# Segment 0 of a recurrent attention runs beside its weight loads, and batched V rows are spread over the segments

## The chip, the cores and the metric

The kernel runs on one core of a Trainium2 chip. The metric is the device time of one execution in microseconds (us); lower is better. The engines are named as in the profile: PE (matrix multiply, with PEld for its weight loads), DVE (vector), ACT (activation), POOL (GpSimd) and SP (which here only issues DMAs).

## What is computed

```python
# A: S = 2048 rows of width 512, in 64 segments of 32; 32 heads of 128; a memory of 8 rows
for s in range(64):
    h = concat(mem, layernorm(x)[s*32:(s+1)*32])            # 40 rows
    q, k, v = h @ Wq, h @ Wk, h @ Wv                          # each 512 -> 32 heads x 128
    p = softmax(where(mask, q @ k.T * 128**-0.5, -1e9))
    o = concat_heads(p @ v) @ Wo                              # 4096 -> 512
    mem, out[s] = o[:8], o[8:]
h = x + out
# B: a gated mixer over all 2048 rows
z = gelu(layernorm(h) @ w_in); z1, z2 = halves(z)
result = h + (z1 * (w_sp @ layernorm(z2) + b_sp)) @ w_out
```

All tensors are bf16. The memory that a segment hands on makes the 64 segments a recurrence.

## The kernel before

**The order of the work.** The program is written out by hand as one list of operations for each engine, by an `Emitter`. `Emitter.add` (L51) derives the waits from the named tokens that an operation reads and writes, and an engine runs its list in program order. Every DMA has a semaphore, and a wait on a DMA is a wait for its landing. For POOL there is one more dependence, on whatever stands before it on POOL:

```python
if eng == "pool" and self.by_eng["pool"]:
    deps.add(self.by_eng["pool"][-1])
```

**The weights.** Wq, Wk, Wv and Wo are 4 MB each and are loaded at the start, in this order, as four transfers of 1 MB each (a quarter holds eight heads), all issued by SP.

**Batched rows.** The last 8 rows of a segment's 32 are handled apart from the 24 rows before them: their q, k and v do not depend on the memory, so they are computed for a chunk of 16 segments at a time (128 rows). `qkx_mm` (L370) makes one group of four heads of q (groups 0 to 7) or k (groups 8 to 15), 16 matmuls of 128x128 into one PSUM bank, and `qkx_evac` (L382) copies it to `QTx`. `vx_mm` (L391) makes one of eight V rows of a chunk, 16 matmuls of which four run side by side, and `vx_evac` (L401) copies it to one of two staging buffers `Vs` and stores it to `vext_d` in DRAM. `load_vx` (L412) brings a segment's part of it back into `Vx` (three buffers). The four chunks hold segments 0 to 15, 16 to 31, and so on; `hTe` holds the transposed, normalized rows of two chunks.

**A segment** (the loop over `s`, L764). `QK` (L430) makes q and k of the 24 fresh rows and the 8 memory rows, 64 matmuls, and ACT and DVE bring them into place; `S_half` (L463) makes the scores with the mask added on PE, needing `qx_copy` (L455), which POOL makes for the next segment; then follow exp on ACT, `V_half` (L525), the sums and the logarithm and second exp that stand for a division, `PV_half` (L542), which needs `Vx`, `cT_evac` (L563), the output projection `Wo` (L575) in two column parts, `part_evac` (L592) and `mem_out` (L596), which puts the new memory into `hT` for the next segment's `QK`. `cTx_copy` (L586) is POOL's. `WoX_mm`, `F_group` and `WoX_scatter` finish a block of four segments one block later. One piece of the transpose of `w_sp` is fetched and written back (`wT_piece`, L669) in every second segment.

**Fillers.** Matmuls of later chunks are put in between. `gx` holds the groups of `qkx_mm`, one per segment, poured ahead of `PV_half`. `gv` holds V rows cut into pieces of four matmuls, four to a row; they are poured in eight of 16 segments (those in `VXS`, L745), one ahead of `Wo`, two ahead of `mem_out`, one behind it.

**The start** (L673 to L714). Two blocks of batched rows (chunks 0 and 1) are loaded first, normalized (`ln_inplace`, L331: two DVE operations, two of POOL, one of DVE) and transposed by PE. The 16 groups of chunk 0 follow as Wq and Wk arrive, with the first two blocks of x loaded, normalized and transposed after group 7, behind `late_consts` (L303), 35 POOL operations that build the mask and other constants. Then come the eight V rows of chunk 0, with stores issued by ACT, the loads of `Vx` for segments 0 and 1, and the segment loop. After the segments the mixer runs, which the change does not touch.

Of the kernel before, what the change touches and what calls it, by code (L numbers as in the profile page):

```python
# [33 lines left out]
class Emitter:  # L34
    ENGS = ("pe", "act", "dve", "pool", "sp")

    def __init__(self, n_dma_sems=16):
        self.ops = []
        self.by_eng = {e: [] for e in self.ENGS}
        self.last_w = {}  # L40
        self.readers = {}
        self.n_dma_sems = n_dma_sems
        self.dma_rr = 0
        self.dma_cnt = [0] * n_dma_sems
        self.dma_last = [None] * n_dma_sems
        self.const_tokens = set()
# [4 lines left out]
    def add(self, eng, fn, reads=(), writes=(), dma=False, after=()):  # L51
        op = _Op(eng, fn)
        deps = set(a for a in after if a is not None)
        for t in reads:
            w = self.last_w.get(t)
            if w is not None:
                deps.add(w)
            if isinstance(t, tuple) and t[0] == "ps":
                for r in self.readers.get(t, ()):
                    if r.eng != eng:  # L60
                        deps.add(r)
        for t in writes:
            w = self.last_w.get(t)
            if w is not None:
                deps.add(w)
            rs = self.readers.get(t)
            if rs:
                deps.update(rs)
        if eng == "pool" and self.by_eng["pool"]:
            deps.add(self.by_eng["pool"][-1])  # L70
        if eng == "pe":
            deps = {d for d in deps if d.eng != "pe" or d.is_dma}
        if dma:
            j = self.dma_rr
            self.dma_rr = (self.dma_rr + 1) % self.n_dma_sems
            op.is_dma = True
            op.dma_sem = j
            self.dma_cnt[j] += 1
            op.dma_val = 16 * self.dma_cnt[j]
            if self.dma_last[j] is not None:  # L80
                deps.add(self.dma_last[j])
            self.dma_last[j] = op
        op.deps = deps
        for t in reads:
            if t in self.const_tokens:
                continue
# [74 lines left out]
def fast_path(nc, st, keep, A_x, A_mem0, A_Wq, A_Wk, A_Wv, A_Wo, A_seg_len, B_w_in, B_w_sp, B_b_sp, B_w_out, out):  # L161
# [45 lines left out]
    hTe = sb("hTe", [128, 2, DC, 128], BF)  # L207
# [69 lines left out]
    def load_x(rb, j):  # L277
        sp(lambda e: e.dma_start(xn[:, j, :], xr[:, rb, :]), writes=[("xn", j)])

    def load_xe(ck, j):  # L280
        sp(lambda e: e.dma_start(xn[:, j, :], xe[CK * ck:CK * ck + CK, XM:SEG, :]), writes=[("xn", j)])
# [9 lines left out]
    load_xe(1, 1)  # L291
    for hq in range(4):
        load_w(0, hq)
    sp(lambda e: e.dma_start(m0[:], A_mem0[0]), writes=["m0"])
# [36 lines left out]
    def ln_inplace(j):  # L331
        dve(lambda e: e.bn_stats(out=st1[:, j, :], in_=xn[:, j, :]), reads=[("xn", j)], writes=[("st1", j)])
        dve(lambda e: e.bn_aggr(out=mv1[:, j, :], in_=st1[:, j, :]), reads=[("st1", j)], writes=[("mv1", j)])
        pool(lambda e: e.tensor_scalar(out=rs1[:, j:j + 1], in0=mv1[:, j, 1:2], scalar1=EPS, scalar2=None, op0=ALU.add),
             reads=[("mv1", j)], writes=[("rs1", j)])
        pool(lambda e: e.tensor_tensor(out=rs1[:, j:j + 1], in0=rs1[:, j:j + 1], in1=mhalf[:, 0:1], op=ALU.pow),
             reads=[("rs1", j), "mhalf"], writes=[("rs1", j)])
        dve(lambda e: e.tensor_scalar(out=xn[:, j, :], in0=xn[:, j, :], scalar1=mv1[:, j, 0:1], scalar2=rs1[:, j:j + 1],
                                      op0=ALU.subtract, op1=ALU.mult),
            reads=[("xn", j), ("mv1", j), ("rs1", j)], writes=[("xn", j)])  # L340

    def xT(j, bank):
        for dc in range(DC):
            pe(lambda e, dc=dc: e.transpose(out=psb[:, bank, dc * 128:(dc + 1) * 128], in_=xn[:, j, dc * 128:(dc + 1) * 128],
                                            identity=ident[:, :]),
               reads=[("xn", j), "ident"], writes=[PB(bank)])
# [10 lines left out]
    def xe_copy(ck, bank):  # L357
        src = psb[:, bank, 0:512].rearrange("p (dc c) -> p dc c", dc=DC)
        act(lambda e: e.activation(out=hTe[:, ck % 2, :, :], in_=src, func=ACT.Copy), reads=[PB(bank)], writes=[("hTe", ck % 2)])
# [10 lines left out]
    def qkx_mm(ck, i, bank, only_hh=None, only_dc=None):  # L370
        mi, h0 = i // 8, 4 * (i % 8)
        ws = (w_q, w_k)[mi]
        for hh in range(4):
            h = h0 + hh
            for dc in range(DC):
                if only_hh is not None and (hh, dc) != (only_hh, only_dc):
                    continue
                pe(lambda e, h=h, dc=dc, hh=hh: e.matmul(ps[:, bank, hh * 128:(hh + 1) * 128], lhsT=ws[:, dc, h * DH:(h + 1) * DH],  # L378
                                                         rhs=hTe[:, ck % 2, dc, :], start=(dc == 0), stop=(dc == DC - 1)),
                   reads=[("hTe", ck % 2), ("W", mi, h // 8)], writes=[PB(bank)])  # L380
# [10 lines left out]
    def vx_mm(ck, n, bank, only=None):  # L391
        for dc in range(DC):
            if only is not None and dc != only:
                continue
            for c in range(4):
                q = slice(32 * c, 32 * c + 32)
                pe(lambda e, dc=dc, c=c, q=q: e.matmul(ps[q, bank, :], lhsT=hTe[:, ck % 2, dc, q], rhs=w_v[:, dc, n * 512:(n + 1) * 512],  # L397
                                                       start=(dc == 0), stop=(dc == DC - 1), tile_position=(0, 32 * c)),
                   reads=[("hTe", ck % 2), ("W", 2, n // 2)], writes=[PB(bank)])

    def vx_evac(ck, n, bank, eng="act", queue="sp"):  # L401
        j = n % 2
        if eng == "act":
            act(lambda e: e.activation(out=Vs[:, j, :], in_=ps[:, bank, :], func=ACT.Copy), reads=[PB(bank)], writes=[("Vs", j)])
# [326 lines left out]
    gx, gv = Gap(), Gap()  # L731

    def qkx_atoms(ck, i):
        mms = [lambda ck=ck, i=i, hh=hh, dc=dc: qkx_mm(ck, i, XB, hh, dc) for hh in range(4) for dc in range(DC)]
        f = lambda: qkx_evac(ck, i, XB, "dve")
        f.eng = "dve"
        gx.add(XB, mms, f)
# [26 lines left out]
    for s in range(NSEG):  # L764
        j4 = s % 4
        rb = s // 4
        ck, i16 = s // CK + 1, s % CK
        if ck < NCK:
            if i16 == 0:
                for n in range(8):  # L770
                    vx_atoms(ck, n)
            qkx_atoms(ck, i16)
# [4 lines left out]
        if s % 2 == 0 and s // 2 < NWT:  # L777
# [3 lines left out]
        if i16 == 11 and 2 <= ck + 1 < NCK:  # L781
            load_xe(ck + 1, 1)
# [22 lines left out]
        sm_rcp(0)  # L805
        V_half(s, 1, (0, 1, 2))
# [12 lines left out]
        ev = gx.pour(16)  # L819
        PV_half(s, 0)  # L820
        PV_half(s, 1)
        cT_evac(0, "act")
# [9 lines left out]
        vx = i16 in VXS  # L832
        late = gv.pour(vx)
# [11 lines left out]
        if i16 == 12 and 2 <= ck + 1 < NCK:  # L845
            ln_inplace(1)
        late += gv.pour(2 * vx)
# [24 lines left out]
    assert not gx.atoms and not gv.atoms  # L872
# [922 lines left out]
```

## Time and profile before

| | us |
|---|---|
| median of 10 runs | 940.42 (938.7 to 943.83) |
| profiled execution, its own time | 940.29 |
| its span | 938.5 |
| PE busy in the span | 881.9 (94%) |
| ACT, DVE, POOL busy | 478.2, 445.3, 108.6 |
| last store of chunk 0's V rows issued | 54.7 |
| first QK of segment 0, 1, 63 | 50.02, 64.11, 745.68 |

The span is that of the profiled execution on the chip. L437 in a line means line 437 of the kernel. Busy time of PE is not work at its peak, since matmuls are pipelined. The chain of waits follows the work that ended last back from the end: it names, at each step, what the next one waited for. The granted clock is the share of full speed that PE was given.

### The profile page before, as it was taken

What the parts mean: (1) busy time and instruction counts of PE and PEld (TensorE: products, weight loads), DVE (VectorE), ACT (ScalarE), POOL (GpSimd) and SP (SyncE); (2) the same over time, 40 slices, a digit from 0 to 9 for tenths busy, and PEclk for the clock granted to TensorE, in tenths of its full rate; (3) what the DMA queues carried; (4) which work ended last, traced back from release to release, by engine and by line L of the source; (5) the groups of instructions that cost most, each with busy time, mean ns of one, the idle gap of its engine ahead of it and who ended that gap; (6) DMA issues with size and microseconds to landing.
All of it is one profiled execution on the core that took longest, in us unless ns stands there. A gap on an engine that the chain in (4) does not pass through costs nothing.

```text
span 938.5 us, 45489 instructions
## 1 busy us (share of the span) xinstructions
PE 881.9 (94%) x20973; PEld 490.7 (52%) x20973; DVE 445.3 (47%) x1029; ACT 478.2 (51%) x1158; POOL 108.6 (12%) x274
## 2 busy tenths in 40 slices
PE   4889999999999999999999999989899999989998
PEld 4545555555555555555555555444444444434443
DVE  3134445555555445555545455444434463453433
ACT  2146566666665666666666666565656565500000
POOL 5001011111111111111111011111101022200000
PEclk9889999999999999999999999999999999999999
DMA  9942012130222222121212130513112193021201
GB/s 330 377 123 68 17 37 66 49 81 24 59 55 57 46 63 46 46 60 38 60 37 66 43 82 18 118 29 79 51 40 62 35 283 119 1 90 41 92 15 36
DMA packets 103668, 71.29 MB, mean 76 GB/s; under 512 B 62248, under 2 KB 89008, under 8 KB 103472
## 3 DMA queue, kind: packets, MB, share of 16 engines
q1 hardware_dynamic: 99248, 67.27, 25.1%
q8 instruction: 166, 2.72, 1.3%
q10 hardware_dynamic: 4224, 1.05, 0.5%
q14 instruction: 30, 0.25, 0.1%
HBM read 39.46 MB, written 18.61 MB: 62 GB/s over the span
## 4 chain that ended last, share of the span: by engine, by line
PE 90%; ACT 4%; DMA 3%; DVE 2%; issue 1%; SPq 0%; POOL 0%; ACTq 0%; POOLq 0%
PE f_ps L437 25%; PE f_ps L581 12%; PE f_ps L531 11%; PE f_ps L938 10%; PE f_ps L378 6%; PE f_ps L625 4%; PE f_ps L900 3%; PE f_ps L548 3%; PE f_ps L931 2%; PE f_ps L1008 2%; PE f_ps L397 2%; PE f_ps L600 2%; PE f_ps L476 2%; DMA vext_d<-f_Vs 1%; PE f_ps L497 1%
## 5 line engine op out<-in xcount | busy, mean ns | idle before, releaser
L437 PE MATMUL f_ps<-f_arena,f_hT 128*32 128x512 bf16 x4096 | 235.8, 383 | 17.6 <-ACT f_hT L603 12.0
L444 ACT ACTIVATE f_Tst<-f_ps 128x512 bf16<-128x512 f32 x256 | 152.6, 597 | 103.4 <-PE f_ps L437 101.3
L437 PEld LDWEIGHTS f_ps<-f_arena,f_hT 128*32 128x32 bf16 x4096 | 104.3, 97 | 128.7 <-ACT f_hT L603 24.2
L531 PE MATMUL f_ps<-f_arena,f_hT 128*32 128x512 bf16 x2048 | 140.1, 378 | 0.0
L450 DVE STREAM_TRANSPOSE f_QT<-f_Tst 128x256 uint32<-128x256 uint32 x128 | 57.0, 446 | 173.7 <-ACT f_Tst L444 173.7
L581 PE MATMUL f_ps<-f_arena,f_cT 128*32 128x384 bf16 (+1 forms) x4096 | 123.5, 273 | 1.5 <-ACT f_cT L567 1.5
L581 PEld LDWEIGHTS f_ps<-f_arena,f_cT 128*32 128x32 bf16 x4096 | 84.9, 97 | 54.9 <-ACT f_cT L567 26.3
L938 PE MATMUL f_ps<-f_arena 128*128 128x512 bf16 x448 | 101.3, 379 | 2.4 <-DVE f_arena L944 1.6
L593 ACT ACTIVATE f_part<-f_ps 128x384 bf16<-128x384 f32 (+1 forms) x128 | 46.4, 384 | 74.4 <-PE f_ps L581 74.3
L453 DVE STREAM_TRANSPOSE f_KT<-f_Tst 128x256 uint32<-128x256 uint32 x128 | 57.0, 445 | 52.7 <-ACT f_Tst L444 52.6
L460 POOL COPY f_QT<-f_arena 128x256 bf16<-128x256 bf16 x64 | 30.7, 480 | 391.6 <-PE f_ps L482 391.6
L569 DVE TENSOR_SCALAR f_cT<-f_ps 128x320 bf16<-128x320 f32 x128 | 56.9, 486 | 38.5 <-PE f_ps L554 38.5
L938 PEld LDWEIGHTS f_ps<-f_arena 128*128 128x128 bf16 x448 | 43.5, 98 | 55.9 <-DVE f_arena L944 2.6
L378 PE MATMUL f_ps<-f_hTe,f_arena 128*128 128x128 bf16 x1024 | 69.7, 226 | 0.5 <-DMA f_arena<-in_A_Wq_dram 0.5
L378 PEld LDWEIGHTS f_ps<-f_hTe,f_arena 128*128 128x128 bf16 x1024 | 61.1, 102 | 12.1 <-issue 12.1
L567 ACT ACTIVATE f_cT<-f_ps 128x320 bf16<-128x320 f32 x128 | 49.0, 435 | 34.6 <-PE f_ps L554 34.6
L517 DVE SCALAR_TENSOR_TENSOR f_E_sb<-f_R_sb,f_E_sb 128x160 bf16<-128x160 f32 x128 | 41.7, 326 | 46.5 <-ACT f_R_sb L513 46.5
L509 ACT ACTIVATE f_R_sb<-f_ps 128x160 f32<-128x160 f32 x128 | 38.8, 303 | 35.8 <-PE f_ps L502 35.8
L531 PEld LDWEIGHTS f_ps<-f_arena,f_hT 128*32 128x32 bf16 x2048 | 44.1, 95 | 21.3
L589 POOL COPY f_cTx<-f_cT 128x256 bf16<-128x256 bf16 x64 | 26.1, 408 | 196.9 <-DVE f_cT L569 196.9
L944 DVE TENSOR_TENSOR f_arena<-f_ps,f_arena 128x512 f32<-128x512 f32 x28 | 19.3, 690 | 57.8 <-PE f_ps L938 57.8
L548 PE MATMUL f_ps<-f_E_sb,f_V_sb 32*128 32x40 bf16 x2048 | 36.1, 178 | 10.4 <-DVE f_E_sb L522 8.9
(95 smaller groups left out, 1088.6 us busy)
## 6 DMA issues: line engine op xcount, KB each, us to landing
wT_d<-f_wst SPq DMA_DIRECT2D x32, 256.0 KB, 2.4
f_arena<-wT_d SPq DMA_DIRECT2D x32, 256.0 KB, 4.4
f_arena<-in_A_Wq_dram SPq DMA_DIRECT2D x4, 1024.0 KB, 8.8
f_arena<-in_A_Wk_dram SPq DMA_DIRECT2D x4, 1024.0 KB, 13.9
f_arena<-in_A_Wv_dram SPq DMA_DIRECT2D x4, 1024.0 KB, 14.5
f_arena<-in_A_Wo_dram SPq DMA_DIRECT2D x4, 1024.0 KB, 15.2
f_Vx<-vext_d SPq DMA_DIRECT2D x64, 64.0 KB, 2.8
vext_d<-f_Vs SPq DMA_DIRECT2D x24, 128.0 KB, 2.0
```

The source lines that it names most:

```text
L378: pe(lambda e, h=h, dc=dc, hh=hh: e.matmul(ps[:, bank, hh * 128:(hh + 1) * 128], lhsT=ws[:, dc, h * DH:(h + 1) * DH], rhs=hTe[:, ck % 2, d ...
L437: pe(lambda e, dc=dc, c=c, rhs=rhs: e.matmul(ps[32 * c:32 * c + 32, bank, :], lhsT=hT[:, sl, dc, :], rhs=rhs, start=(dc == 0), stop=(dc == ...
L444: act(lambda e: e.activation(out=Tst[:, tb, :].rearrange("p (hp i r) -> p hp i r", i=32, r=2), in_=ps[:, bank, :].rearrange("p (hp r i) -> ...
L450: dve(lambda e: e.transpose(out=dst, in_=src), reads=[("T", tb)], writes=[("QT", b)])
L453: dve(lambda e: e.transpose(out=dst, in_=src), reads=[("T", tb)], writes=[("KT", b)])
L531: pe(lambda e, dc=dc, c=c, c0=c0: e.matmul(ps[32 * c:32 * c + 32, bank, :], lhsT=hT[:, sl, dc, :], rhs=w_v[:, dc, c0:c0 + 512], start=(dc ...
L548: pe(lambda e, q=q, c=c, g=g, c0=c0: e.matmul(ps[:, PVB[c], c0:c0 + 40], lhsT=V_sb[q, b, g * 128:(g + 1) * 128], rhs=E_sb[q, b, g * 40:(g ...
L567: act(lambda e: e.activation(out=dst, in_=src, func=ACT.Copy, scale=UNSC), reads=[PB(PVB[c])], writes=[("cT", c)])
L569: dve(lambda e: e.tensor_scalar(out=dst, in0=src, scalar1=UNSC, scalar2=None, op0=ALU.mult), reads=[PB(PVB[c])], writes=[("cT", c)])
L581: pe(lambda e, h=h, g=g, i=i, b=b, c=c: e.matmul(ps[32 * g:32 * g + 32, bank, 0:d1 - d0], lhsT=cTh[:, i, 8:40], rhs=w_o[:, h, d0:d1], star ...
L593: act(lambda e: e.activation(out=part[:, s % 8, d0:d1], in_=ps[:, bank, 0:d1 - d0], func=ACT.Copy), reads=[PB(bank)], writes=[("part", s % ...
L938: pe(lambda e: e.matmul(ps[:, bank, 0:TB], lhsT=z2[:, sc, fb * 128:(fb + 1) * 128], rhs=wTb[tb % 2][:, :, sc, :], start=(sc == 0), stop=(s ...
```

## The change

The rows of x and of the batched blocks are loaded behind Wq (the first block still ahead of it), now three batched blocks of which the third is chunk 2's; those that have no room in `xn` go into `part`, which holds the segments' outputs later. The normalizations stand after groups 5 and 7, `late_consts` after them on POOL. Four q groups of chunk 1 go between chunk 0's k groups. The V rows of chunk 0 move into segment 0: two ahead of `S_half`, two behind it, four behind the second exp. Each is evacuated into a slot of `part` of its own and stored from ACT's queue (even rows) or POOL's (odd rows), whose DMAs get four semaphores of their own. `load_vx` for segments 0 and 1 goes to POOL, behind `qx_copy(1)`. Four more q groups of chunk 1 stand in segment 0, two ahead of `PV_half` and two behind it. The fillers `gx` become one list of whole groups: V rows of chunk 1 in segments 0 to 7, then chunk 1's k groups, then chunks 2 and 3. The pieces `gv` are those of chunks 2 and 3, one ahead of `mem_out` in two of four segments and one behind it in every segment. `wT_piece` moves to the odd segments.

```diff
...
         if dma:
-            j = self.dma_rr
-            self.dma_rr = (self.dma_rr + 1) % self.n_dma_sems
+            if eng == "pool":
+                self.sw_rr = (self.sw_rr + 1) % 4
+                j = self.n_dma_sems - 4 + self.sw_rr
+            else:
+                j = self.dma_rr
+                self.dma_rr = (self.dma_rr + 1) % (self.n_dma_sems - 4)
...
-    hTe = sb("hTe", [128, 2, DC, 128], BF)
+    hTe = sb("hTe", [128, 3, DC, 128], BF)
...
+    def xbuf(j):
+        return (xn[:, j, :], [("xn", j)]) if j < 2 else (part[:, j, :], [("part", j, 0), ("part", j, 1)])
...
     load_xe(0, 0)
-    load_xe(1, 1)
     for hq in range(4):
         load_w(0, hq)
+    load_xe(1, 1)
+    load_x(0, 4)
+    load_x(1, 5)
+    load_xe(2, 6)
...
-        j = n % 2
+        if ck == 0:
+            t, tok = part[:, n, :], [("part", n, 0), ("part", n, 1)]
+        else:
+            j = vcnt[0] % 2
+            vcnt[0] += 1
+            t, tok = Vs[:, j, :], [("Vs", j)]
         if eng == "act":
-            act(lambda e: e.activation(out=Vs[:, j, :], in_=ps[:, bank, :], func=ACT.Copy), reads=[PB(bank)], writes=[("Vs", j)])
+            act(lambda e: e.activation(out=t, in_=ps[:, bank, :], func=ACT.Copy), reads=[PB(bank)], writes=tok)
         else:
-            dve(lambda e: e.tensor_copy(out=Vs[:, j, :], in_=ps[:, bank, :]), reads=[PB(bank)], writes=[("Vs", j)])
+            dve(lambda e: e.tensor_copy(out=t, in_=ps[:, bank, :]), reads=[PB(bank)], writes=tok)
         b, c = n // 4, n % 4
         dst = vext_d[ck, 4 * c:4 * c + 4, :, b * DH:(b + 1) * DH].rearrange("g t e -> t g e")
-        em.add(queue, lambda e: e.dma_start(dst, Vs[:, j, :].rearrange("p (g e) -> p g e", g=4)), dma=True, reads=[("Vs", j)],
+        em.add(queue, lambda e: e.dma_start(dst, t.rearrange("p (g e) -> p g e", g=4)), dma=True, reads=tok,
                writes=[("vext", ck, n)])
...
-    def load_vx(s):
+    vcnt = [0]
+
+    def load_vx(s, queue="sp"):
         i = s % CK
-        sp(lambda e: e.dma_start(Vx[:, s % NVX, :, :], vext_d[s // CK, :, 8 * i:8 * i + 8, :]),
-           reads=[("vext", s // CK, n) for n in range(8)], writes=[("Vx", s % NVX)])
+        em.add(queue, lambda e: e.dma_start(Vx[:, s % NVX, :, :], vext_d[s // CK, :, 8 * i:8 * i + 8, :]), dma=True,
+               reads=[("vext", s // CK, n) for n in range(8)], writes=[("Vx", s % NVX)])
...
     act(lambda e: e.preload_act_table_set("natural_log_exp_and_others"))
-    for j in range(2):
-        ln_inplace(j)
-        xT(j, 6 + j)
-        xe_copy(j, 6 + j)
-    load_x(0, 0)
-    load_x(1, 1)
+    ln_inplace(0)
+    xT(0, 6)
+    xe_copy(0, 6)
     for hq in range(4):
         load_w(1, hq)
-    late_consts()
-    ebank = (0, 1, 2, 3)
-
-    def start_group(cnt, mm, ev, *a):
+    ebank = (2, 3, 4, 5)
+    scnt = [0]
+
+    def start_group(mm, ev, *a):
+        cnt = scnt[0]
+        scnt[0] += 1
         bk = ebank[cnt % 4]
         mm(*a, bk)
-        ev(*a, bk, "act" if cnt % 2 == 0 else "dve")
+        eng = "act" if cnt % 2 == 0 else "dve"
+        if mm is vx_mm:
+            ev(*a, bk, eng, {"act": "act", "dve": "pool"}[eng])
+        else:
+            ev(*a, bk, eng)
+
+    def start_x(ck, i):
+        start_group(qkx_mm, qkx_evac, ck, i)
+
+    def start_v(n):
+        start_group(vx_mm, vx_evac, 0, n)
 
     for i in range(16):
-        start_group(i, qkx_mm, qkx_evac, 0, i)
+        start_x(0, i)
+        if i == 5:
+            ln_inplace(1)
+            ln_inplace(4)
         if i == 7:
-            for j in range(2):
-                ln_inplace(j)
-                xT(j, 6 + j)
-                ring_copy(j, 6 + j)
-            mem0_transpose(5)
+            ln_inplace(5)
+            ln_inplace(6)
+            late_consts()
+        if i == 8:
+            xT(1, 7)
+            xe_copy(1, 7)
+        if i == 10:
+            xT(4, 6)
+            ring_copy(0, 6)
+        if i == 12:
+            xT(5, 7)
+            ring_copy(1, 7)
+        if i == 14:
+            xT(6, 6)
+            xe_copy(2, 6)
+            mem0_transpose(7)
+        if i >= 9 and i % 2 == 1:
+            start_x(1, i // 2 - 4)
     for hq in range(4):
         load_w(2, hq)
     wor = A_Wo.rearrange("h e d -> e h d")
     for hq in range(4):
         sp(lambda e, hq=hq: e.dma_start(w_o[:, 8 * hq:8 * hq + 8, :], wor[:, 8 * hq:8 * hq + 8, :]), writes=[("Wo", hq)])
         em.mark_const(("Wo", hq))
-    for n in range(8):
-        bk = ebank[n % 4]
-        vx_mm(0, n, bk)
-        vx_evac(0, n, bk, "act" if n % 2 == 0 else "dve", "act")
-    for s in range(2):
-        load_vx(s)
...
-    gx, gv = Gap(), Gap()
-
...
+    def qkx_group(ck, i):
+        def f():
+            qkx_mm(ck, i, XB)
+            return lambda: qkx_evac(ck, i, XB, "dve")
+        gx.append(f)
+
+    def vx_group(ck, n):
+        def f():
+            vx_mm(ck, n, XB)
+            return lambda: vx_evac(ck, n, XB, "dve")
+        gx.append(f)
 
     def vx_atoms(ck, n):
         mms = [lambda ck=ck, n=n, dc=dc: vx_mm(ck, n, VXB, dc) for dc in range(DC)]
-        f = lambda: vx_evac(ck, n, VXB, "act")
-        f.eng = "act"
-        gv.add(VXB, mms, f)
-
-    VXS = (0, 1, 4, 5, 7, 8, 9, 12)
+        gv.add(VXB, mms, lambda: vx_evac(ck, n, VXB, "act"))
+
+    for n in range(8):
+        vx_group(1, n)
+    for ck, i0 in ((1, 8), (2, 0), (3, 0)):
+        for i in range(i0, 16):
+            qkx_group(ck, i)
+    for ck in (2, 3):
+        for n in range(8):
+            vx_atoms(ck, n)
...
-        ck, i16 = s // CK + 1, s % CK
-        if ck < NCK:
-            if i16 == 0:
-                for n in range(8):
-                    vx_atoms(ck, n)
-            qkx_atoms(ck, i16)
         if j4 == 1 and rb > 0:
             load_h(rb - 1)
         if s == NSEG - 1:
             load_h(rb)
-        if s % 2 == 0 and s // 2 < NWT:
+        if s % 2 == 1 and s // 2 < NWT:
             wT_piece(s // 2)
         if j4 == 0 and 2 <= rb + 2 < RB:
             load_x(rb + 2, 0)
-        if i16 == 11 and 2 <= ck + 1 < NCK:
-            load_xe(ck + 1, 1)
+        if s == 4:
+            load_xe(3, 1)
 
...
             load_wT(0, [lastop["q"]])
+        if s == 0:
+            for n in range(2):
+                start_v(n)
         S_half(s, 0)
         sm_exp(0)
+        if s == 0:
+            for n in range(2, 4):
+                start_v(n)
         V_half(s, 0)
         V_evac(0, "dve")
...
         sm_rcp(0)
+        if s == 0:
+            for n in range(4, 8):
+                start_v(n)
         V_half(s, 1, (0, 1, 2))
...
-        ev = gx.pour(16)
+        if s == 0:
+            for j in range(2):
+                load_vx(j, "pool")
+            for i in range(4, 6):
+                start_x(1, i)
+        ev = [gx.pop(0)()] if gx else []
         PV_half(s, 0)
         PV_half(s, 1)
+        if s == 0:
+            for i in range(6, 8):
+                start_x(1, i)
...
-        vx = i16 in VXS
-        late = gv.pour(vx)
+        late = []
         Wo((0, 2, 1, 3), OB, 0, OC)
...
-        if i16 == 12 and 2 <= ck + 1 < NCK:
+        if s == 5:
             ln_inplace(1)
-        late += gv.pour(2 * vx)
+        if j4 < 2:
+            late += gv.pour(1)
         if j4 == 2 and 2 <= rb + 2 < RB:
             xT(0, XB)
             late.append(lambda: ring_copy(rb + 2, XB))
-        if i16 == 13 and 2 <= ck + 1 < NCK:
+        if s == 9:
             xT(1, XB)
-            late.append(lambda: xe_copy(ck + 1, XB))
+            late.append(lambda: xe_copy(3, XB))
         if s + 1 < NSEG:
             mem_out(s)
-        late += gv.pour(vx)
+        late += gv.pour(1)
...
```

`ln_inplace`, `xT`, `load_x` and `load_xe` take their buffer from `xbuf`, and `hTe` is indexed by `ck % 3`; these edits are left out above.

More of the change, by code (lines that the diff above doesn't have):

```diff
@@ L43, in __init__ @@
         self.dma_rr = 0
+        self.sw_rr = 0
         self.dma_cnt = [0] * n_dma_sems
@@ L277, in load_x @@
     def load_x(rb, j):
-        sp(lambda e: e.dma_start(xn[:, j, :], xr[:, rb, :]), writes=[("xn", j)])
+        t, tok = xbuf(j)
+        sp(lambda e: e.dma_start(t, xr[:, rb, :]), writes=tok)
+    def xbuf(j):
+        return (xn[:, j, :], [("xn", j)]) if j < 2 else (part[:, j, :], [("part", j, 0), ("part", j, 1)])
     def load_xe(ck, j):
-        sp(lambda e: e.dma_start(xn[:, j, :], xe[CK * ck:CK * ck + CK, XM:SEG, :]), writes=[("xn", j)])
+        t, tok = xbuf(j)
+        sp(lambda e: e.dma_start(t, xe[CK * ck:CK * ck + CK, XM:SEG, :]), writes=tok)
     def load_w(mi, hq):
@@ L331, in ln_inplace @@
     def ln_inplace(j):
[L332 to L340, printed above, removed]
+        t, tok = xbuf(j)
+        k = j % 2
+        dve(lambda e: e.bn_stats(out=st1[:, k, :], in_=t), reads=tok, writes=[("st1", k)])
+        dve(lambda e: e.bn_aggr(out=mv1[:, k, :], in_=st1[:, k, :]), reads=[("st1", k)], writes=[("mv1", k)])
+        pool(lambda e: e.tensor_scalar(out=rs1[:, k:k + 1], in0=mv1[:, k, 1:2], scalar1=EPS, scalar2=None, op0=ALU.add),
+             reads=[("mv1", k)], writes=[("rs1", k)])
+        pool(lambda e: e.tensor_tensor(out=rs1[:, k:k + 1], in0=rs1[:, k:k + 1], in1=mhalf[:, 0:1], op=ALU.pow),
+             reads=[("rs1", k), "mhalf"], writes=[("rs1", k)])
+        dve(lambda e: e.tensor_scalar(out=t, in0=t, scalar1=mv1[:, k, 0:1], scalar2=rs1[:, k:k + 1], op0=ALU.subtract, op1=ALU.mult),
+            reads=tok + [("mv1", k), ("rs1", k)], writes=tok)
     def xT(j, bank):
+        t, tok = xbuf(j)
         for dc in range(DC):
-            pe(lambda e, dc=dc: e.transpose(out=psb[:, bank, dc * 128:(dc + 1) * 128], in_=xn[:, j, dc * 128:(dc + 1) * 128],
+            pe(lambda e, dc=dc: e.transpose(out=psb[:, bank, dc * 128:(dc + 1) * 128], in_=t[:, dc * 128:(dc + 1) * 128],
                                             identity=ident[:, :]),
-               reads=[("xn", j), "ident"], writes=[PB(bank)])
+               reads=tok + ["ident"], writes=[PB(bank)])
     def slot(s):
@@ L358, in xe_copy @@
         src = psb[:, bank, 0:512].rearrange("p (dc c) -> p dc c", dc=DC)
-        act(lambda e: e.activation(out=hTe[:, ck % 2, :, :], in_=src, func=ACT.Copy), reads=[PB(bank)], writes=[("hTe", ck % 2)])
+        act(lambda e: e.activation(out=hTe[:, ck % 3, :, :], in_=src, func=ACT.Copy), reads=[PB(bank)], writes=[("hTe", ck % 3)])
     def mem0_transpose(bank):
@@ L378, in qkx_mm @@
                 pe(lambda e, h=h, dc=dc, hh=hh: e.matmul(ps[:, bank, hh * 128:(hh + 1) * 128], lhsT=ws[:, dc, h * DH:(h + 1) * DH],
-                                                         rhs=hTe[:, ck % 2, dc, :], start=(dc == 0), stop=(dc == DC - 1)),
-                   reads=[("hTe", ck % 2), ("W", mi, h // 8)], writes=[PB(bank)])
+                                                         rhs=hTe[:, ck % 3, dc, :], start=(dc == 0), stop=(dc == DC - 1)),
+                   reads=[("hTe", ck % 3), ("W", mi, h // 8)], writes=[PB(bank)])
     def qkx_evac(ck, i, bank, eng="act"):
@@ L396, in vx_mm @@
                 q = slice(32 * c, 32 * c + 32)
-                pe(lambda e, dc=dc, c=c, q=q: e.matmul(ps[q, bank, :], lhsT=hTe[:, ck % 2, dc, q], rhs=w_v[:, dc, n * 512:(n + 1) * 512],
+                pe(lambda e, dc=dc, c=c, q=q: e.matmul(ps[q, bank, :], lhsT=hTe[:, ck % 3, dc, q], rhs=w_v[:, dc, n * 512:(n + 1) * 512],
                                                        start=(dc == 0), stop=(dc == DC - 1), tile_position=(0, 32 * c)),
-                   reads=[("hTe", ck % 2), ("W", 2, n // 2)], writes=[PB(bank)])
+                   reads=[("hTe", ck % 3), ("W", 2, n // 2)], writes=[PB(bank)])
     def vx_evac(ck, n, bank, eng="act", queue="sp"):
-        j = n % 2
+        if ck == 0:
[4 more added lines that the diff above has]
+            t, tok = Vs[:, j, :], [("Vs", j)]
         if eng == "act":
-            act(lambda e: e.activation(out=Vs[:, j, :], in_=ps[:, bank, :], func=ACT.Copy), reads=[PB(bank)], writes=[("Vs", j)])
+            act(lambda e: e.activation(out=t, in_=ps[:, bank, :], func=ACT.Copy), reads=[PB(bank)], writes=tok)
         else:
-            dve(lambda e: e.tensor_copy(out=Vs[:, j, :], in_=ps[:, bank, :]), reads=[PB(bank)], writes=[("Vs", j)])
+            dve(lambda e: e.tensor_copy(out=t, in_=ps[:, bank, :]), reads=[PB(bank)], writes=tok)
         b, c = n // 4, n % 4
         dst = vext_d[ck, 4 * c:4 * c + 4, :, b * DH:(b + 1) * DH].rearrange("g t e -> t g e")
-        em.add(queue, lambda e: e.dma_start(dst, Vs[:, j, :].rearrange("p (g e) -> p g e", g=4)), dma=True, reads=[("Vs", j)],
+        em.add(queue, lambda e: e.dma_start(dst, t.rearrange("p (g e) -> p g e", g=4)), dma=True, reads=tok,
                writes=[("vext", ck, n)])
-    def load_vx(s):
+    vcnt = [0]
+    def load_vx(s, queue="sp"):
         i = s % CK
-        sp(lambda e: e.dma_start(Vx[:, s % NVX, :, :], vext_d[s // CK, :, 8 * i:8 * i + 8, :]),
-           reads=[("vext", s // CK, n) for n in range(8)], writes=[("Vx", s % NVX)])
+        em.add(queue, lambda e: e.dma_start(Vx[:, s % NVX, :, :], vext_d[s // CK, :, 8 * i:8 * i + 8, :]), dma=True,
+               reads=[("vext", s // CK, n) for n in range(8)], writes=[("Vx", s % NVX)])
     QKB = {(0, 0): 0, (0, 1): 1, (1, 0): 6, (1, 1): 7}
@@ L729, in pour @@
             return done
-    gx, gv = Gap(), Gap()
[L733 to L737, printed above, removed]
+    gx, gv = [], Gap()
+    def qkx_group(ck, i):
[8 more added lines that the diff above has]
+        gx.append(f)
     def vx_atoms(ck, n):
         mms = [lambda ck=ck, n=n, dc=dc: vx_mm(ck, n, VXB, dc) for dc in range(DC)]
-        f = lambda: vx_evac(ck, n, VXB, "act")
-        f.eng = "act"
-        gv.add(VXB, mms, f)
-    VXS = (0, 1, 4, 5, 7, 8, 9, 12)
+        gv.add(VXB, mms, lambda: vx_evac(ck, n, VXB, "act"))
[7 more added lines that the diff above has]
+            vx_atoms(ck, n)
     wTb = [region(0, RB * 512).rearrange("p (t sc c) -> p t sc c", sc=RB, c=64),
@@ L871, in fast_path @@
         px = lastop.get("x")
-    assert not gx.atoms and not gv.atoms
+    assert not gx and not gv.atoms
     lastQ, lastK, lastV = lastop["q"], lastop["k"], lastop["v"]
```

## Prediction

> **What bounds the kernel now.** I read the chain of waits first, for the first 120 us. Columns: start us, length us, what the end waited for.
>
> ```profile
> 3.89 11.98 DMA f_arena<-in_A_Wq_dram
> ...
> 33.62 1.01 PE f_ps L397 x16
> 34.65 0.61 ACT f_Vs L404
> 35.28 6.36 DMA vext_d<-f_Vs
> 41.72 0.61 ACT f_Vs L404
> 42.35 6.94 DMA vext_d<-f_Vs
> 49.37 0.61 ACT f_Vs L404
> 50.02 1.90 PE f_ps L437 x15
> 51.92 4.77 PE f_ps L437 x44
> ...
> 60.83 0.43 ACT f_cT L567
> 61.30 1.93 PE f_ps L581 x64
> 63.23 0.43 PE f_ps L397 x7
> 63.86 0.21 ACT f_hT L603
> 64.11 3.64 PE f_ps L437 x64
> ```
>
> From 35.28 to 50 the path is the two-buffer V staging waiting for its own stores. Segment 0 begins at 50.02, its output projection (Wo, L581) at 61.30, segment 1 at 64.11. Next, the windows (us, then busy time of PE, PEld, DVE, ACT, POOL, the granted clock, DMA share, GB/s):
>
> ```profile
> 46.00:48.00 2.00, 0.10 (x4) 0.00 (x0) 0.00 (x0) 0.00 (x0) 0.00 (x0) 1.00 1.13 356
> 50.00:52.00 2.00, 1.98 (x20) 0.55 (x24) 0.69 (x1) 0.00 (x0) 0.00 (x0) 0.50 0.58 162
> ```
>
> The DMA engines are full from 4 to about 51 us, and after an idle gap PE runs at a granted clock of 0.50: segment 0's QK takes 6.67 us for the 3.64 of every other segment. Third, the DMA issues in the stretch 42.3 to 43, where the last column is us to landing:
>
> ```profile
> f_arena<-in_A_Wo_dram SPq DMA_DIRECT2D x1, 1024.0 KB, 12.5
> vext_d<-f_Vs ACTq DMA_DIRECT2D x1, 128.0 KB, 6.9
> ```
>
> So a V store takes 6.4 to 7.3 us while weights stream (the four issued at 35 to 44) and 1.9 to 2.4 once they have landed (the four at 50 to 55). The last Wo quarter, issued at 39.4, lands at 51.9. Last, the segments of the chain, segment 7 and then a segment with no filler:
>
> ```profile
> 140.06 0.22 PE f_ps L610 x4
> 140.27 0.22 PE f_ps L635 x4
> 140.49 0.43 PE f_ps L397 x7
> ...
> 632.36 0.21 issue
> 632.57 0.23 DVE f_E_sb L522
> ```
>
> A segment takes 10.95 to 11.0 us with four V pieces, 10.95 without, and still 10.91 after segment 48, where even the 1.00 us QK filler is gone: the recurrence sets the period and fillers lie in its waits. The exceptions are segments 7, 23 and 39 (11.67, 11.42, 11.41): there F (L610) and the scatter (L635) already fill the wait before the memory output, and the two V pieces (0.43) come on top.
>
> **The even spread.** Segments 7, 23 and 39 lose their excess over segment 11's 10.97: 0.70 + 0.45 + 0.44 = 1.6 us. Two of three segments now carry one V piece (0.22) ahead of the memory output, where segment 3 waits 0.50 for L593; one follows it, beside 0.27 of waiting. Both are hidden; uncovered, a piece costs 0.22. Chunk 1's V as the filler of segments 0 to 7 is 0.86 of PE for 1.00, worth at most 0.05 a segment. Together −1.8 us.
>
> **The start, up to the V rows.** The x loads go behind Wq and change places with a load ahead of it: the bytes ahead of Wk are the same, so its quarters still land at 20.3 to 28.0. Four normalizations on DVE, one after another from 16.0 at 2.3 us each, end near 25.5; only evacuations queue behind them, and banks 2 to 5 cover that. The 11.2 us of constants on POOL then run from 25.2 to 36.4, qx_copy to 36.9, which S needs near 39.6: hidden, with 2.7 us to spare. PE stands from 17.6 to 20.3, shorter than the 3.2 to 3.9 us of idling after which the clock fell in the windows (at 21.9, 42.4 and 49.2); then eight K groups and four of chunk 1 at 1.0, 1.9 of transposes, QK 3.64: 37.8. V rows 0 and 1 (0.86 each) end at 39.6, and DVE evacuates row 1 by 40.4. The rows have a slot each, so no evacuation waits for a store.
>
> **The V stores on two queues.** This is the step that decides. The emitter makes every POOL operation depend on the POOL operation before it, and if that was a DMA the wait is for its landing. So the odd stores go one at a time: 1, 3, 5, 7, then qx_copy(1), then the load of Vx for segment 0. The trace has no DMA from POOL; ACT's stores are the nearest rows. Store 1 from 40.4 takes 6.8: 47.2. Store 3, again beside the weights (which end near 52.5, as more V stores share the engines than before): 54.0. Stores 5 and 7 at 2.2: 58.4. The copy is 0.6, the load 2.5 (its row: 2.3 to 2.8): Vx is there at T = 61.5. ACT's own even stores leave by 46.5 and land before 53.
> Bounds for T: were each store 1.9 and the evacuations the pace, PE's own work, which ends near 52, is the end, so T = 53. With 3.4 per store (the longest off the loaded stretch), 3.1 for the load and a V row that comes 0.5 later, 65. I take the middle, by the ACT rows.
> PE has nothing else after 52 (the chunk 1 groups 4 and 5, the V filler): PV waits for T. Behind PV in program order stand chunk 1's groups 6 and 7, then Wo. PE has idled 8 us, so they run at half clock: 1.8 us each, as the first two K groups did from 24.16. T + 0.5 (PV) + 3.6 + 2.4 (Wo 1.93, its start still slow) + 0.9 (to the next QK, as from 63.23 to 64.11) = T + 7.4 = 68.9 against 64.11: +4.8. A T of 65 gives +8.3; at T = 56 it is −0.7, and at 53, with a warm clock, 53 + 0.5 + 2.0 + 1.9 + 0.9 = 58.3: −5.8.
>
> **The skill beside it.** The Trainium skill, DMA: Bandwidth & Descriptors, section Rules for kernel authors, says that spreading DMAs over SP, ACT and GpSimd saves issue time only, as they share the engines. The rows agree on the sharing (6.9 beside a Wo transfer, 2.0 alone); the issue time saved is 0.37 a store, four times, off the path. The same page's section on the anatomy of a GpSimd DMA fits 2.0 us plus bytes over 436e3; by that estimate a store takes 2.3, the evacuations become the pace, T is near 54, and the outcome is that of the second rival below.
> TensorE: Matmul & The Clock Gate, Part 1, gives about 3.4 us of sustained work to warm up. This trace has 0.50 for 6 us from 50.0 and for some 4 us from 24.2. By the rule the cost after T would be 1.7 us, by the rows up to 3.
>
> **The sum.** Profiled execution: span 938.5, its own time 940.29, so 1.8 outside the span; the median of ten is 940.42. Start +4.8, spread −1.8: +3.0, so 943.3 profiled and 943.4 as a median. The later segments and the tail are as before: the last piece of w_sp moves from segment 62 to 63, and SP, waiting there only for its own buffer, issues it early.
>
> **Rivals.** (A) The forecast: POOL's serial stores hold Vx until T of 59.5 to 64, start +2.8 to +7.3, 941.5 to 946. (B) The stores from POOL are quick even beside the weights, being one more queue that the engines serve, and T is 53 to 56.5: start −5.8 to −0.2, with the spread −7.6 to −2.0, so 932.8 to 938.4; it decides from T under 56.7. For it: PE's own work ends at 52 and the last Wo quarter near 52.5, so nothing else is later. Against: all four rows under load are above 6.4. (C) T of 56.7 to 59.5: what the spread gives, the start takes, 938.5 to 941.4. (D) Each DMA from POOL costs a microsecond that ACT's rows do not have (no row bounds it above): five more, T 65 to 67, 946.9 to 948.9.
>
> **Chances.** A 0.45, B 0.27, C 0.14, D 0.14. About 0.2% (1.9 us) is what a measurement of this kernel can tell from no change; some 0.09 of A lies within that, all of C, none of D. Faster 0.27, same 0.23, slower 0.50. The range, 936.0 to 947.5, leaves out about 0.1 of B on one side and 0.1 of D on the other; A's own is 941.5 to 946.
>
> **What would show it.** Right: four stores from POOL in single file, Vx(0) landing near 61, PE idle before PV of segment 0 and at 0.50 behind it, segment 1's QK near 69; segments 7, 23, 39 at 10.95 to 11.0. Wrong: POOL's stores overlapping or under 4 us beside Wo; QK of segment 1 before 62; S of segment 0 waiting for the constants; or later segments whose period moves by more than 0.1.

## The result and the profile after

The changed kernel takes 945.56 us (median of 12 runs, 944.13 to 947.42) beside 941.14 (40 runs, 938.7 to 945.49): a ratio of 1.0043, 95% interval 1.0032 to 1.0054. It is slower by 4.4 us. The profiled execution took 944.75 with a span of 943.0, so 4.5 us more span than before.

The chain of waits of the changed kernel from 38 to 70 us (start us, length us, what the end waited for):

```profile
42.09 0.86 PE f_ps L554 x16
...
48.31 5.45 DMA vext_d<-f_part
...
54.28 2.23 DMA vext_d<-f_part
...
57.04 0.75 POOL vext_d L430
57.79 1.51 issue
59.30 0.04 POOLq L154
59.35 0.46 POOL f_QT L483
59.80 0.29 issue
60.09 2.18 DMA f_Vx<-vext_d
62.27 0.05 issue
62.31 0.24 PE f_ps L577 x4
62.55 0.13 PE f_ps L571 x16
62.69 0.05 PE f_ps L577 x4
62.74 3.54 PE f_ps L394 x32
66.28 0.02 issue
66.31 0.69 DVE f_arena L405
67.00 0.41 DVE f_cT L592
67.41 0.04 issue
67.45 1.61 PE f_ps L604 x56
...
69.93 2.12 PE f_ps L460 x33
```

Up to 48 us segment 0 is ahead of where it was: its V (L554) starts at 42, where before its QK had not begun. Then one POOL store follows another, the copy, and the load of Vx, which PV (L577) gets at 62.3. Behind it come the two groups of chunk 1 at half speed (3.54 for 32 matmuls; 2.0 at full clock), the evacuation of the second ahead of cT on DVE, Wo (56 of its 64 matmuls; eight had run at 66.2, inside the wait for DVE), and segment 1's QK at 69.93 (64.11 before). POOL's own timeline (start, length, engine, line, what; in brackets the idle time before it and who ended it):

```profile
41.19 1.01 POOL L430 DMA_DIRECT2D vext_d<-f_part  x1 [4.17 <-DVE f_part L427]
48.31 0.77 POOL L430 DMA_DIRECT2D vext_d<-f_part  x1 [6.11 <-DVE f_part L427]
54.28 0.75 POOL L430 DMA_DIRECT2D vext_d<-f_part  x1 [5.20 <-DMA vext_d<-f_part]
57.04 0.75 POOL L430 DMA_DIRECT2D vext_d<-f_part  x1 [2.00 <-DMA vext_d<-f_part]
```

The second store is put down to DVE, but its row had been evacuated at 42.8: a wait for several semaphores is given to the one that came last by the records, and what was there to wait for is the landing of the first store, 6.6 us after 41.19. The windows show the clock (the columns are us, five engines, granted clock, DMA share, GB/s):

```profile
54.00:56.00 2.00, 0.00 (x0) 0.00 (x0) 0.00 (x0) 0.00 (x0) 0.75 (x1) 1.00 0.16 66
60.00:62.00 2.00, 0.00 (x0) 0.00 (x0) 0.00 (x0) 0.00 (x0) 0.57 (x1) 0.50 0.12 33
65.00:66.00 1.00, 1.00 (x12) 1.00 (x10) 0.00 (x0) 0.85 (x3) 0.00 (x0) 0.50 0.00 0
```

From 54 to 62 no engine but POOL has work, and the DMA engines are nearly idle too.

Where the 4.5 us are, by the first QK of segments 1 and 63 in the two chains:

| | before | after | difference | forecast |
|---|---|---|---|---|
| up to QK of segment 1 | 64.11 | 69.93 | +5.8 | +4.8 |
| segments 1 to 62 | 681.57 | 679.16 | −2.4 | −1.8 |
| from QK of segment 63 | 192.82 | 193.91 | +1.1 | 0 |

### The profile page after: what moved, and what is told of

It reads as the page before. It is cut to its first block, busy times and chain, and to the rows that moved or that the text cites. A ratio compares the mean times of both kernels' runs of the same rounds, so it can differ in the third digit from the quotient of the medians.

```text
span 943.0 us, 45485 instructions
## 1 busy us (share of the span) xinstructions
PE 887.6 (94%) x20973; PEld 489.1 (52%) x20973; DVE 447.4 (47%) x1033; ACT 476.1 (50%) x1154; POOL 113.5 (12%) x280
## 4 chain that ended last, share of the span: by engine, by line
PE 90%; ACT 3%; DMA 2%; issue 2%; DVE 1%; SPq 1%; POOL 0%; POOLq 0%
PE f_ps L460 25%; PE f_ps L604 12%; PE f_ps L554 11%; PE f_ps L1002 10%; PE f_ps L394 6%; PE f_ps L648 4%; PE f_ps L964 3%; PE f_ps L571 3%; PE f_ps L995 2%; PE f_ps L1072 2%; PE f_ps L623 2%; PE f_ps L413 2%; PE f_ps L499 2%; ACT f_hT L626 1%; PE f_ps L520 1%
## 5 line engine op out<-in xcount | busy, mean ns | idle before, releaser
L554 PE MATMUL f_ps<-f_arena,f_hT 128*32 128x512 bf16 x2048 | 140.4, 378 | 0.0
L554 PEld LDWEIGHTS f_ps<-f_arena,f_hT 128*32 128x32 bf16 x2048 | 45.0, 95 | 21.5
L405 DVE CAST f_arena<-f_ps 128x512 bf16<-128x512 f32 x52 | 35.5, 683 | 30.3 <-PE f_ps L394 30.3
```

The costliest lines, as they stand in the source:

```text
L554: pe(lambda e, dc=dc, c=c, c0=c0: e.matmul(ps[32 * c:32 * c + 32, bank, :], lhsT=hT[:, sl, dc, :], rhs=w_v[:, dc, c0:c0 + 512], start=(dc ...
```

## The experiments

Line numbers differ between the kernels. "QK of segment 1" is where its first matmul starts; the time is the median, and ratios are to the kernel before, run on the same chip.

**No wait between POOL's DMAs** (the changed kernel with this edit).

```diff
-        if eng == "pool" and self.by_eng["pool"]:
-            deps.add(self.by_eng["pool"][-1])
+        if eng == "pool":
+            prev = [o for o in self.by_eng["pool"] if not o.is_dma]
+            if prev:
+                deps.add(prev[-1])
```

> The changed kernel, but an operation of POOL depends on the last POOL operation that is not a DMA, so POOL's four stores need not land one after another. Serial theory (the stores wait for each other): stores 3, 5 and 7 leave as soon as their rows are evacuated (43, 46, 48) and land by 54; Vx(0) lands at 56 to 57 instead of 62.3, segment 1's QK starts near 63.5 instead of 69.9, the span falls by about 6 us to near 937. Rival, the POOL queue is slow by itself (each DMA costs its time whether waited for or not): Vx(0) stays after 60, the span falls by under 2 us. Rival, the last Wo quarter holds segment 0: no change.

Measured: 938.64 us, ratio 0.9970 (0.9959 to 0.9981); span 938.7. POOL's timeline:

```profile
42.78 0.77 POOL L432 DMA_DIRECT2D vext_d<-f_part  x1 [0.95 <-DVE f_part L429]
45.68 0.75 POOL L432 DMA_DIRECT2D vext_d<-f_part  x1 [2.13 <-DVE f_part L429]
47.52 0.75 POOL L432 DMA_DIRECT2D vext_d<-f_part  x1 [1.09 <-DVE f_part L429]
```

Stores leave as their rows are there, each landing after 5.9 to 6.5 us; PV has Vx at 56.8, and QK of segment 1 starts at 64.76 instead of 69.93. The queue is not slow by itself; the wait is. Vx came where it was expected (56 to 57), QK of segment 1 later than the 63.5 expected, by what stands behind Vx. The chain now runs over the last store of ACT:

```profile
46.19 7.87 DMA vext_d<-f_part
...
54.68 2.09 DMA f_Vx<-vext_d
```

**Groups 6 and 7 of chunk 1 ahead of PV** (the changed kernel; `range(4, 6)` becomes `range(4, 8)` and the second loop goes).

> The changed kernel with chunk 1's groups 6 and 7 ahead of PV of segment 0 instead of behind it, where PE idles. Serial theory: Vx(0) still lands near 62.3; behind it 3.5 us of the two groups at half clock and 1.1 of DVE (group 7's evacuation ahead of the cT evacuations) leave the path, but the half clock then falls on Wo and QK: segment 1's QK at 67 to 68.5 instead of 69.9, span lower by 1.5 to 3 us. Rival, the groups are the cause of the loss: segment 1's QK falls by the whole 4.6 us or more, to 65.3 or below.

Measured: 943.26 us, ratio 1.0010 (0.9999 to 1.0021), so 2.3 us better than the changed kernel, and 2.2 at QK of segment 1. Vx is there at 62.33, as before the edit, and QK of segment 1 starts at 67.73. Chain:

```profile
62.80 0.43 ACT f_cT L590
63.23 0.04 issue
63.28 3.61 PE f_ps L604 x64
```

4.6 us of groups and evacuation left the path, but the cT evacuation on ACT (0.43) came in, and Wo took 3.61, where it takes 1.93 at full clock: the half clock that followed the idle time fell on it (granted clock 0.50 from 58 to 66). Work moved into a wait gave back its own length less what the half clock took from the work behind it.

**A slot for each V row, nothing else** (the kernel before; `vx_evac` for chunk 0 takes `part[:, n, :]` instead of `Vs[:, n % 2, :]`).

> The kernel before with one edit: each V row of chunk 0 is evacuated into a slot of its own (those of the changed kernel) instead of two staging buffers; all stores stay with ACT, the order of the work stays. If the staging wait alone is what the start loses: the V rows end near 41, segment 0's QK starts near 41 instead of 50.0, Vx(0) lands near 51, Wo runs from about 53 as the last Wo quarter lands (51.9 before, later by the stores), segment 1's QK starts at 56 to 57 instead of 64.1; span lower by 7 to 8 us than the kernel before, near 931. If the weights themselves were the limit: segment 1's QK stays above 60 and the gain is under 4 us.

Measured: 938.91 us, ratio 0.9962 (0.9948 to 0.9977); span 937.4. QK of segment 0 starts at 40.96 as expected, but QK of segment 1 only at 61.0. ACT's timeline shows what took the place of the staging wait:

```profile
34.70 1.38 ACTq L412 DMA_DIRECT2D vext_d<-f_part  x2
36.75 1.00 ACTq L412 DMA_DIRECT2D vext_d<-f_part  x2
38.42 3.19 ACTq L412 DMA_DIRECT2D vext_d<-f_part  x2
42.29 3.81 ACTq L412 DMA_DIRECT2D vext_d<-f_part  x2
46.15 2.26 ACT L447 ACTIVATE f_Tst<-f_ps 128x512 bf16<-128x512 f32 x4 [3.89 <-issue]
```

The first four issues take 0.37 to 0.42 us; from the fifth on, with four or more stores under way on the queue, one takes 1.2 to 2.6. ACT stands in it, and the evacuation of segment 0's first q, ready near 42, comes at 46.15. The stores land 6.4 to 11.7 us after issue, the last six 9.2 or more. QK of segment 1 above 60 is the number of the rival, but not for its reason: the last Wo quarter was there at 53.4, Vx only at 55.7.

**The same with the odd stores on POOL** (no wait between POOL's DMAs, and four semaphores of their own for them, as in the changed kernel).

> The kernel before with a slot for each V row of chunk 0, as in the run with slots alone, and the odd stores on POOL's queue without a wait between them. In the run with slots alone ACT's eight stores took up to 2.0 us each to issue (0.37 when the queue is empty), ACT stood in them until 46.1 and segment 0's first q came 4 us late. If ACT's full queue is the cause: with four stores each, ACT is free by 43, segment 0's S near 45 instead of 47.8, the stores land by 50 instead of 53.6, segment 1's QK at 56 to 57.5 instead of 61.1, time about 4 us under that run, near 934.5. Rival, the engines are simply full and the stores land at 53 to 54 either way: QK of segment 1 stays within 1 us of 61.1.

Measured: 937.32 us, ratio 0.9966 (0.9953 to 0.9979); span 933.1. ACT's issues are 0.37 to 0.39 again, the first q is evacuated at 42.37, the stores land by 49.0 instead of 53.6. So eight stores on one queue were the cause of the ACT wait, and here a second queue gains time at the start. The rest of the expectation failed: QK of segment 1 starts at 59.27, 1.7 us earlier and not 4, and the ratios of the two runs (0.9962 and 0.9966) do not tell them apart. The next wait is the load of Vx, which SP now issues while the weights still stream:

```profile
41.27 7.76 DMA vext_d<-f_part
49.03 0.02 SPq L156
49.05 0.04 issue
49.09 4.68 DMA f_Vx<-vext_d
```

It takes 4.68 us instead of 2.1 to 2.2, and Wo behind it again starts at half clock (3.19). The last Wo quarter landed at 53.5, so a quicker load would soon have met that limit.

**Both edits on the changed kernel** (no wait, groups 6 and 7 first).

> The changed kernel with both edits: no POOL operation waits for a DMA of POOL's before it, and chunk 1's groups 6 and 7 ahead of PV of segment 0. Serial theory with the groups as the second term: Vx(0) lands at 56.8 as in the run without the wait; PE idles only 2 us before it, so the clock stays up, and the path behind it is 0.5 + 0.5 + 1.9 + 0.9: segment 1's QK at 60.5 instead of 64.8, the time 4 us under that run, near 934.5. Rival, the last Wo quarter becomes the limit: QK of segment 1 not below 62.5.

Measured: 936.81 us, ratio 0.9959 (0.9946 to 0.9972). Vx at 57.5, QK of segment 1 at 62.77: a number of the rival's (not below 62.5), but not for its reason, as the chain goes over the store and the last Wo quarter was there at 54.6, before Vx. What failed is that the clock would stay up: PE stood 3.8 us before PV's last part, not 2, and Wo took 3.56 us.

**The V rows early** (as the last, and all eight groups of chunk 1 behind the V rows; the edit is shown against the changed kernel, without the two edits of the last run that it keeps).

```diff
-        if i >= 9 and i % 2 == 1:
-            start_x(1, i // 2 - 4)
...
-            for i in range(4, 6):
+            for i in range(0, 8):
                 start_x(1, i)
```

> As the run before (no wait on POOL's DMAs), and all eight q groups of chunk 1 stand behind the V rows in segment 0, so the V rows follow QK of segment 0 as their weights land (31 to 39 us). The last V row is evacuated near 42 instead of 47.5, its store lands near 49, Vx(0) near 52, and Wo begins when its last quarter is there, near 53: segment 1's QK at 56.5 to 58, time near 931. If the landing of the stores is set by the end of the weight stream (52 to 54) whenever they leave: Vx(0) stays near 56.5, QK of segment 1 near 60.5, the time equal to that of the run before.

Measured: 934.47 us, ratio 0.9937 (0.9924 to 0.9951): the fastest of all, by 0.6% below the kernel before. The chain of waits:

```profile
43.59 8.04 DMA vext_d<-f_part
...
52.25 2.21 DMA f_Vx<-vext_d
...
54.92 0.43 ACT f_cT L592
55.36 0.04 issue
55.40 1.93 PE f_ps L606 x64
...
58.21 1.90 PE f_ps L462 x29
```

Vx is there at 54.5 (expected 52, as the last ACT store took 8.0 us). PE works on chunk 1 until shortly before, the clock is up, and Wo takes 1.93. The stores land earlier when they leave earlier, so the end of the weight stream did not set them. Little is left to gain that way: the last Wo quarter landed at 53.7.

**All eight stores on POOL** (the last kernel with one line changed).

> The kernel with the V rows early and no wait between POOL's DMAs, but all eight V stores on POOL's queue. Beside the weight stream POOL's stores landed after 5.5 to 6.5 us, ACT's after 7.4 to 8.4, and the last to land was ACT's sixth row (43.6 + 8.0). If the queue makes that difference: the last store lands about 50.5 instead of 51.6, Vx(0) at 53.4 instead of 54.5, segment 1's QK at 57.0 to 57.5 instead of 58.2, a gain of up to 1 us. If eight stores on one queue hold each other up, as ACT's eight did (landing 9.8 to 11.7): Vx(0) at 56 or later, 1 to 3 us slower. If the last Wo quarter ends last by then: QK of segment 1 unchanged.

Measured: 939.06 us, ratio 0.9969 (0.9955 to 0.9982); QK of segment 1 at 61.91. The stores took 5.7 to 7.0 us each, as before; but only four semaphores serve POOL's DMAs, so the fifth store waited for the first's landing, until 44.0, and the seventh for the third's, until 46.9, and the last landed at 53.9. Vx came 2.2 us later than in the run before, at 56.7; the other 1.5 us are Wo (3.43), at half clock after PE had stood for only 2.4 us. So the experiment mixed the queue with its semaphores, and whether POOL's queue alone would be better with eight stays open.

**One V row of each chunk elsewhere** (the kernel before; `VXS` with 6 instead of 7).

> The kernel before with one number changed: the V row of segments 7, 23 and 39 is made in segments 6, 22 and 38. If those three segments lose their excess because F and the scatter already fill the wait: their periods fall from 11.67, 11.42 and 11.41 to 10.95 to 11.0, segments 6, 22, 38 stay at 11.0, the span falls by 1.4 to 1.6 us. If the excess comes with the V row wherever it stands: no change in sum.

Measured: 941.13 us, ratio 0.9999 (0.9988 to 1.0009). Segments 7, 23 and 39 fell to 10.97, but segments 6, 22 and 38 rose to 11.43, 11.40 and 11.41. The chain of segment 6 says why:

```profile
128.12 0.43 PE f_ps L397 x8
128.55 0.33 PE f_ps L344 x4
128.88 0.25 PE f_ps L600 x16
```

There the transposes of x (L344) stand in the same wait, and with two V pieces ahead of them the wait is overfull too.

**All V rows in segments whose number modulo 4 is 0 or 1** (the kernel before; `VXS` is 0, 1, 4, 5, 8, 9, 12, 13).

> The kernel before with the V rows of segments 7 and 12 of each 16 moved so that all stand in segments whose number modulo 4 is 0 or 1 (0, 1, 4, 5, 8, 9, 12, 13). Moving 7 to 6 moved the excess along (11.43, 11.40, 11.41 in 6, 22, 38), so the refined theory is: the excess belongs to segments where other work (transposes in the third, F and the scatter in the fourth of a block) already fills the wait ahead of the memory output. Then no segment of 0 to 47 but 13 and 29 (which have both transposes of the next chunk and a V row) is above 11.1, and the time from the QK of segment 1 to that of segment 63 falls from 681.6 to about 680.6. Rival, a V row of four pieces costs 0.4 once in eight rows wherever it stands: no change in that sum.

Measured: 940.06 us, ratio 0.9993 (0.9983 to 1.0003). The periods agree with the refined theory where the rows were moved: 7, 23 and 39 are at 10.97, and 13 and 29, with transposes and a V row, at 11.40 and 11.41. But the time from QK of segment 1 to that of segment 63 did not fall: it was 681.82, after 681.57 before. Segment 1 took 11.62, and segments 24 and 25 together 0.5 us more than usual, with PE standing for nothing that the profile shows; in segment 1:

```profile
63.35 0.83 PE f_ps L437 x11
64.18 0.31 issue
64.49 3.08 PE f_ps L437 x53
```

These three segments had a V row in the kernel before too (10.95, 10.99 and 11.07 there), so the move of the rows does not explain them. The gain of about 1 us that was expected is seen in the moved segments and not in the sum, and the whole time cannot tell it from nothing.

## Why the prediction was right

The forecast was 943.4 us, slower by 3.0; measured was slower by 4.4, within its range. The side and the mechanism held; each size came out a little differently, and that some sums came out close is luck, as said below.

**POOL's single file.** The step that decided was right, and shown by the run without the wait: 5.2 us at QK of segment 1, 6.9 us in the median. Vx was put at 61.5 and came at 62.3. The stores took 6.6, 5.5, 2.2 and 2.2 where 6.8, 6.8, 2.2 and 2.2 were taken from ACT's rows, and the load 2.2 for 2.5; the sum leaves out about 0.5 us between a landing and the next store's issue on POOL, three times, and 0.3 ahead of the load. Of these 1.9 us and the 0.8 by which the first store left late, quicker transfers and a shorter copy made up 1.9: that T came within 0.8 is in part luck. The rival with quick POOL stores (B) fell: they are no faster than 5.4 us beside the weights. Of the five extra microseconds of rival D, the 1.9 between POOL's DMAs are what showed. The first store left at 41.2 for a forecast of 40.4: Wk's first quarter was there at 21.0, not 20.3. One step before it was wrong without harm: PE stood for 3.6 us up to 21.2 and did drop to a granted clock of 0.50 (22.2 to 25.7); the groups and transposes still took 13.6 us for a forecast of 13.9.

**Behind Vx.** T + 7.4 was forecast, T + 7.6 measured, but out of other parts. The step that is wrong is the share of Wo: 2.4 was put for a cold start, and 1.6 is what stood on the path, at full clock, with eight of the 64 matmuls already done. Missing is DVE: group 7's evacuation (0.69) stands ahead of the cT evacuations, and Wo waits 1.1 us for both. That the errors nearly cancel is luck.

**The clock.** The granted clock was 0.50 until about 66.6 in this trace, 4.3 us after PV, and the two groups took 3.54. By the 3.4 us of sustained work that the Trainium skill gives (TensorE: Matmul & The Clock Gate, Part 1) the clock would have risen at about 65.7, which is estimated to make the groups shorter by some 0.25 us. The row differs from that, as the clock was still 0.50 from 65 to 66, but at this place the difference is small.

**The spread.** Right in size for segments 7, 23 and 39: 11.67, 11.42 and 11.41 became 10.93, 10.97 and 10.97, 1.6 us. The reason given was too narrow: the excess is not that of F and the scatter alone, but comes wherever other work stands in the wait ahead of the memory output, as the runs with moved rows show. The changed kernel puts no piece ahead of the memory output there; it has one in two of four segments, where the prediction says two of three. Segments 1 to 6, with the shorter filler, lost 0.3 in all, about the 0.05 each that was forecast at most. One of the prediction's own signs of being wrong did show, a later period that moves by more than 0.1. Segment 9, with transposes and a piece, went from 11.00 to 11.15, and 11.14 to 11.15 in every run built on the changed kernel. Segment 18 went from 10.96 to 11.17 (11.04 to 11.39 in those runs), partly with PE standing inside PV for nothing that the profile shows; why is open. Segments 25 (11.07, then 10.95), 47 (11.20, then 10.97) and 52 (10.97, then 11.19) moved too, but read otherwise in runs with the same work there, so the change was not shown to cause it. The rest of the −2.4, some 0.7, is spread over many segments.

**The tail.** Forecast 0, measured +1.1; 0.49 of it is one stretch inside segment 63's Wo in which PE waited for nothing shown. The tail goes with the clock over all profiles, with the same mixer work: in the stretch of 20 us that holds the end of the first mixing, the granted clock was 1.00 in the profiles of the kernel before, the changed one, the V rows early, and the slots with two queues, and their tails are 192.8 to 193.9; it was 0.91 in all seven others, and theirs are 194.6 to 196.1. So spans of single profiles differ by up to 3 us in a part that no edit touches. The kernel before and the changed one are both in the first group, so this does not explain their 1.1; no edit was shown to cause it, and the rest of it stays open.

**The rule that spreading DMAs over queues does not help bandwidth and only saves issue time** (the Trainium skill, DMA: Bandwidth & Descriptors, Rules for kernel authors) was taken as harmless here. On bandwidth the runs with slots agree: the last Wo quarter landed at 53.4 with eight stores on ACT and at 53.5 with four on each of two queues. But the stores themselves, beside SP's weights, landed by 53.6 in the one and by 49.0 in the other. And the issue time was up to 2.6 us, on an engine with other work.

## What to carry to other kernels

Before a transfer moves to another queue, read what the program makes that queue wait for: an order kept for an engine's own operations turns into one landing after another once DMAs stand among them. Ask also what the receiving engine does besides; with four or more stores under way on its queue, a store cost ACT up to 2.6 us here. Work that fills a wait is free only up to the wait's length. And an idle time of PE can make the work behind it dearer: where Wo came next, it took 1.93 us when PE had stood for 0.2 us (the V rows early), and 2.7 to 3.6 when PE had stood for 2.4 to 9 us.

## What the runs showed of the hardware

- A store issued on ACT took 0.37 to 0.46 us with up to three others under way and 1.2 to 2.6 with four or more, beside a weight stream; POOL's issues took 0.75 to 1.0 and did not grow with three others under way.
- Beside the stream of weights, POOL's stores of 128 KB landed after 5.4 to 7.0 us, ACT's after 6.5 to 8.4 with four on the queue and 6.4 to 11.7 with eight (the last six 9.2 or more); POOL's took 2.2 without the stream.
- The load of 64 KB for segment 0 took 4.68 us issued on SP at 49 us, beside the last of the weights, and 2.1 to 2.2 us issued at 52 to 60 us (on POOL, or on SP at 53.6 in the run with slots alone). Whether POOL's queue would have been quicker at 49 was not tried.
- The granted clock was 0.50 behind an idle time of PE of 2.4 us (all stores on POOL, 54.3 to 56.7) as well as behind one of 9.2 us (the changed kernel).
- The same mixer work, from QK of segment 63 on, took 192.8 to 193.9 us in the four profiles in which the granted clock stayed at 1.00 in one stretch of 20 us, and 194.6 to 196.1 in the seven in which it was 0.91 there.
